# Moving the first batch's sink product from VectorE to GpSimd

## The chip, the core and the metric

The kernel runs on one core of one Trainium2 chip. A core has five engines that run side by side, each through its own list of instructions in order: TensorE (PE, matmuls; its weight loads are listed as PEld), VectorE (DVE), ScalarE (ACT), GpSimd (POOL) and SyncE (SP, here only issuing transfers). Engines wait for one another and for transfers (DMAs) by semaphores. The metric is the device time of one execution in microseconds; the lower, the better.

## The reference

Two stages, one behind the other. Attention with a sliding window and sink keys, for q, k and v of 4 batches, 8 heads, 768 positions and 64 elements a head:

```python
scores = scale * np.matmul(q, k.transpose(0, 1, 3, 2))
is_sink = pos[None, :] < int(n_sink)            # n_sink = 4
rel = pos[:, None] - pos[None, :]
in_window = (rel >= 0) & (rel < int(window))    # window = 128
keep = is_sink | in_window
scores = np.where(keep, scores, -1000000000.0)
a = np.exp(scores - max); a = a / (sum + 1e-09)
return np.matmul(a, v)
```

Then, on the heads put side by side (x: 4 x 768 rows of 512), a normalised two-layer network with a residual:

```python
xn = (x - mu) / np.sqrt(var + 1e-06) * g_ln
ch = np.maximum(xn @ w_ch1, 0.0) @ w_ch2        # 512 -> 2048 -> 512
return x + ch
```

## The kernel before

Rows are worked on in 24 tiles of 128 (six for each batch); two tiles make a chunk, so there are 12 chunks of 256 rows. For each chunk, k and q are loaded in natural layout, transposed, and multiplied to scores that hold keys along partitions (L679 in the first two chunks, L726 behind them); ScalarE takes the exponential (L685, L740), VectorE multiplies it with the window's mask (L688, L744; the first three tiles have the mask added on TensorE, L665), and TensorE multiplies with v (L774). v carries a column of ones, so that the 65th column of the product is the sum of the weights. VectorE takes its reciprocal (L787), scales (L789, which gives x), takes mean and variance (L793, L795) and subtracts the mean (L797, "centering": xc). xc is transposed (L810 on TensorE in the first three chunks, by DMA later), multiplied by the gain (L821) and goes through the first layer (L836 for chunk 0, tile by tile, in groups of 16 matmuls; L843 from chunk 1 on), a ReLU (L853 or L855) and the second layer (L872). L880 multiplies with the row's 1/sqrt(var), which GpSimd computes (L802, L803), and adds x.

The four sink keys of each head get their own small product from the second tile pair of a batch on: L693 (L730 later) multiplies q with a matrix of sink keys, ScalarE takes the exponential (L696, L748: the tile ps), and L769 multiplies it with vs, which has for each batch and head the sink rows of v in the rows that belong to that head, and zero in the others. vs is the product at L506. Its sources are vc, which holds the sink rows of v for all batches and a column of ones (eight small loads issued by SP at L502 fill it), and sel, the head selector: for each of 128 rows, which of 8 heads it belongs to. Both are read with stride 0 in one dimension, so that 128 x 65 and 128 x 8 values give 128 x 520. L506 is made four times, once for each batch; vs0 is needed first by tile 2's L769.

The order of the work isn't written out by hand. Each piece is entered with `P.op(name, {engine: (occupied, until ready)}, priority, ...)`; a planner (`Plan.run`) plays the pieces through with these costs, and each engine takes, of what can start within a small window, the piece of lowest priority. `nb` is a time before which a piece doesn't start; `dma` gives costs for a transfer and puts it on one of eight lanes of a planned queue. A piece with two engines goes to the one that would end it first: so the planner chooses where the transposed k and q are copied out of PSUM (L547, VectorE or ScalarE). The resulting order is emitted engine by engine. A change of one cost can therefore move other pieces; it does so in this case.

GpSimd's list around the place of the change: it issues the loads of the first chunks (L593, L541), the four quarters of the first layer's weights w1 (L514), the loads of chunk 2 (L627), the first two with k and the next two with q, and the quarters of the second layer's weights w2 (L517), with the rescales L802 and L803 of tiles 0 to 3 between them. A transfer issued by GpSimd waits until the one eight places before it has landed.

The priorities that the change touches are these lines, and the functions follow:

```python
P.op(f"vcd{h}", {"SP": (0.3, 0.3)}, 3.2 + 0.01 * h, ..., dma=HW_T)
P.op(f"vs{b}", {"DVE": dve(520)}, 2.0 if b == 0 else 48.0 * b - 20, ..., nb=12.0 if b == 0 else 40.0 * b)
```

Of the kernel before, what the change touches and what calls it, by code (L numbers as in the profile page):

```python
# [206 lines left out]
def dve(n, per=1.04):  # L207
    t = 0.067 + 0.001 * per * n
    return (t, t + 0.09)


def fix(occ, extra=0.09):
# [9 lines left out]
HW_T = (0.10, 0.8, 0.8)  # L222
# [3 lines left out]
NEVER = -1e9  # L226

PAR = dict(strict=40.0, win=0.4, tr=-8.0, sc=-5.0, sc1=-2.0, av=2.0, trx=9.0, by_dma=4, x_by_dma=3,
           w1p=(1.6, 2.6, 2.7, 2.8), pm=3, w2p=(4.5, 4.51, 4.52, 4.53), apart=2, by_tile=1, vp=(0.0, 0.1, 2.0, 2.1, 4.55, 4.56), ld1=0.05)


def general(tc, nc, slots, pairs, ones, ident_f, ident, w1, w2, mhalf, g_s, g_r, q, k, v, out, scale):
# [126 lines left out]
def kernel(  # L359
# [12 lines left out]
    nc = tc.nc  # L372
# [19 lines left out]
    P = Plan()  # L392
# [25 lines left out]
    def const(name, shape, dtype):  # L418
        return consts.tile(shape, dtype, name=name)
# [5 lines left out]
    sel = const("sel", [128, H], FP32)  # L425
    vc = const("vc", [128, B, 65], FP32)
    vs = [const(f"vs{b}", [128, H, 65], BF16) for b in range(B)]
# [11 lines left out]
    Bc = {n: Buf(n) for n in names}  # L439
    Bvs = [Buf(f"vs{b}") for b in range(B)]  # L440
# [6 lines left out]
    V, G = nc.vector, nc.gpsimd  # L447
# [35 lines left out]
    def negs(e):  # L483
# [15 lines left out]
         writes=[Bc["gt"]], dma=HW_T)  # L499
    for h in range(H):  # L500
        p0 = 32 * (h // 2) + NS * (h % 2)
        P.op(f"vcd{h}", {"SP": (0.3, 0.3)}, 3.2 + 0.01 * h, lambda e, h=h, p0=p0: nc.sync.dma_start(  # L502
            vc[p0:p0 + NS, :, 0:64], v[:, h, 0:NS, :].rearrange("b s d -> s b d")),
            reads=[Bc["vc"]], writes=[Bc["vcd"]], dma=HW_T)
    for b in range(B):
        P.op(f"vs{b}", {"DVE": dve(520)}, 2.0 if b == 0 else 48.0 * b - 20, lambda e, b=b: V.tensor_tensor(  # L506
            vs[b], vc[:, b, :].unsqueeze(1).to_broadcast([128, H, 65]),
            sel.unsqueeze(2).to_broadcast([128, H, 65]), op=ALU.mult),
            reads=[Bc["vcd"], Bc["vc"], Bc["sel"]], writes=[Bvs[b]], nb=12.0 if b == 0 else 40.0 * b)

    w1prio = PAR["w1p"]
    for c in range(4):
# [3 lines left out]
    for c in range(4):  # L516
        P.op(f"w2ld{c}", {"POOL": (0.75, 0.8)}, PAR["w2p"][c], lambda e, c=c: G.dma_start(  # L517
            w2[c], moe_w_ch2[512 * c:512 * (c + 1), :].rearrange("(t p) n -> p t n", p=128)),
            writes=[Bw2[c]], dma=SW_W)
# [376 lines left out]
    for c in range(NC):  # L896
        mlp(c)
        if c == PAR["x_by_dma"] - 1:
            for s in range(4):
                for j in range(NDM):  # L900
                    P.op(f"w1g{s}{j}", {"DVE": fix(0.26)}, 16.0 * c + 11.0 + 2 * s + 0.1 * j,
                         lambda e, s=s, j=j: V.tensor_scalar_mul(w1[s][:, j, :], w1[s][:, j, :], gt[:, j:j + 1]),
                         reads=[Bw1[s], Bc["gt"]], writes=[Bw1g[s]], after=last_use[s])

    def guard(e):
# [8 lines left out]
         reads=[pt_f], writes=[fl_b])  # L914
# [67 lines left out]
```

## Time and profile before

| what | value |
|---|---|
| runs: median (lowest to highest of 3) | 222.38 us (221.90 to 223.41) |
| the profiled execution's own time | 222.43 us |
| its span (first to last instruction) | 220.8 us |
| PE busy | 212.1 us (96%) |
| PEld busy | 144.6 us (65%) |
| DVE busy | 117.2 us (53%) |
| ACT busy | 108.8 us (49%) |
| POOL busy | 89.8 us (41%) |
| granted TensorE clock | 0.998 |
| L506 on DVE, 4 instructions | 0.68 to 0.70 us each |

The profile is that of one execution; its time is the span and 1.6 us around it. Busy times add up what each engine's instructions took; an engine that is busy half of the span may still be the one that all others wait for in some stretch. The page cuts the span into 40 slices of 5.5 us and gives each engine's busy share in tenths. "Idle before, releaser" behind a row says how long the engine stood still ahead of it and what ended that. Start times are counted from the start of the span. Rows of neighbouring instructions overlap a little, since an engine starts one before it has fully ended the last.

### The profile page before, as it was taken

To read this page: it belongs to the slowest core of one execution; us is meant where nothing else is said; L and a number is where in the kernel's file an instruction comes from. 1 tells how busy PE (TensorE), PEld (TensorE's weight loads), DVE (VectorE), ACT (ScalarE), POOL (GpSimd) and SP (SyncE) were. 2 spreads that over 40 slices of the span, in tenths; PEclk is the share of its full clock that TensorE was granted. 3 is DMA by queue.
4 is the path that set the end of the run, shared out by engine and by line. 5 is a ranking of instruction groups with operands and counts; after the bars stand their busy time and mean duration, and the time that the engine had idled before them with its cause. 6 is when DMAs were issued, how large, how long until landed. Compare 5 with 4: busy or idle time off the path is not lost.

```text
span 220.8 us, 5072 instructions
## 1 busy us (share of the span) xinstructions
PE 212.1 (96%) x2033; PEld 144.6 (65%) x2033; DVE 117.2 (53%) x269; ACT 108.8 (49%) x163; POOL 89.8 (41%) x130
## 2 busy tenths in 40 slices
PE   6888999999999999999999999999999999999991
PEld 2556975764964964964955965965955955966861
DVE  5499745585796725725706815716706706722011
ACT  3767565145546447445546546445545546531700
POOL 7987663798073480760460741740110110120000
PEclk9999999999999999999999999999999999999999
DMA  5999999999999896999997997998713511111012
GB/s 158 160 184 206 177 207 193 155 211 149 175 171 141 137 146 110 149 127 119 143 124 119 143 118 121 130 123 111 129 38 80 136 28 47 59 39 72 23 52 62
DMA packets 108576, 27.45 MB, mean 124 GB/s; under 512 B 99201, under 2 KB 105601, under 8 KB 108545
## 3 DMA queue, kind: packets, MB, share of 16 engines
q0 software_dynamic: 74944, 13.11, 79.6%
q1 hardware_dynamic: 32400, 13.28, 29.4%
q10 hardware_dynamic: 1200, 0.66, 1.1%
q8 instruction: 18, 0.29, 0.6%
q14 instruction: 14, 0.11, 0.1%
HBM read 27.30 MB, written 6.29 MB: 152 GB/s over the span
## 4 chain that ended last, share of the span: by engine, by line
PE 90%; DVE 4%; DMA 2%; ACT 1%; issue 1%; DVEq 0%
PE one L872 39%; PE one L843 35%; PE pair L726 5%; PE pair L774 4%; PE one L836 2%; DMA natf<-in_k_dram 2%; PE pair L769 1%; DVE st L793 1%; DVE x L789 1%; PE one L632 1%; PE one L576 1%; PE one L730 1%; PE pair L665 1%; DVE xnt L821 1%; DVE xc L797 1%
## 5 line engine op out<-in xcount | busy, mean ns | idle before, releaser
L872 PE MATMUL one<-w,h 128*128 128x512 bf16 (+1 forms) x400 | 89.0, 371 | 0.0
L853 ACT ACTIVATE h<-one 128x512 bf16<-128x512 f32 x95 | 56.8, 598 | 59.3 <-PE one L843 54.2
L843 PE MATMUL one<-xnt,w 128*128 128x256 bf16 x704 | 82.4, 273 | 0.0
L843 PEld LDWEIGHTS <-w 128*128 128x128 bf16 x704 | 67.4, 98 | 10.2
L872 PEld LDWEIGHTS <-h 128*128 128x128 bf16 x400 | 37.4, 98 | 38.6 <-issue 2.0
L744 DVE TENSOR_TENSOR pe<-pe,mask 128x1024 bf16<-128x1024 bf16 (+1 forms) x40 | 26.0, 650 | 55.6 <-ACT pe L740 54.7
L740 ACT ACTIVATE pe<-pair 128x1024 bf16<-128x1024 f32 (+1 forms) x40 | 36.2, 957 | 34.1 <-PE pair L726 31.8
L618 POOL DMA_DIRECT2D nat<-in_k_dram x16 | 14.3, 893 | 39.6 <-DMA kT<-nat 29.7
L880 DVE SCALAR_TENSOR_TENSOR ot<-one,st,x 128x512 f32<-128x512 f32 (+1 forms) x25 | 18.2, 726 | 22.6 <-PE one L872 22.4
L802 POOL TENSOR_SCALAR st<-st 128x1 f32<-128x1 f32 x24 | 7.5, 313 | 43.2 <-DVE st L795 42.1
L541 POOL DMA_DIRECT2D vn<-in_v_dram x24 | 21.9, 920 | 3.7 <-DMA w<-in_moe_w_ch_dram 3.1
L618 POOL DMA_DIRECT2D nat<-in_q_dram x16 | 14.8, 926 | 11.7 <-DMA qT<-nat 8.5
L793 DVE BATCH_NORM_STATS2 st<-x 128x6 f32<-128x512 bf16 x24 | 16.7, 695 | 0.8
L774 PEld LDWEIGHTS <-pe 128*128 128x128 bf16 x352 | 14.0, 97 | 2.3 <-ACT pe L685 0.6
L803 POOL TENSOR_TENSOR st<-st,mhalf 128x1 f32<-128x1 f32 x24 | 14.2, 593 | 2.0
L789 DVE TENSOR_TENSOR x<-pair,rec 128x512 bf16<-128x512 f32 x20 | 13.8, 691 | 0.7
L726 PEld LDWEIGHTS <-kT 64*128 64x128 bf16 x216 | 6.9, 94 | 8.5 <-issue 8.3
L774 PE MATMUL pair<-vn,pe 128*128 128x65 bf16 x296 | 12.2, 193 | 0.0
L726 PE MATMUL pair<-qT,kT 64*128 64x128 bf16 (+1 forms) x216 | 11.6, 238 | 0.0
L797 DVE TENSOR_SCALAR xc<-x,st 128x512 bf16<-128x512 bf16 x24 | 9.1, 377 | 0.9
L787 DVE RECIPROCAL rec<-pair 128x8 f32<-128x8 f32 x20 | 4.1, 204 | 9.9 <-PE pair L774 9.9
L685 ACT ACTIVATE pe<-pair 128x1024 bf16<-128x1024 f32 (+1 forms) x8 | 7.2, 918 | 3.6 <-PE pair L679 3.6
(84 smaller groups left out, 123.3 us busy)
## 6 DMA issues: line engine op xcount, KB each, us to landing
out_dram<-ot SPq DMA_DIRECT2D x23, 256.0 KB
w<-in_moe_w_ch_dram POOLq DMA_DIRECT2D x8, 512.0 KB, 12.3
vn<-in_v_dram POOLq DMA_DIRECT2D x24, 128.0 KB, 6.1
nat<-in_k_dram POOLq DMA_DIRECT2D x22, 128.0 KB, 5.8
nat<-in_q_dram POOLq DMA_DIRECT2D x22, 128.0 KB, 5.0
natf<-in_k_dram SPq DMA_DIRECT2D x2, 256.0 KB
natf<-in_q_dram ACTq DMA_DIRECT2D x2, 256.0 KB
xnt<-xc SPq DMA_TRANSPOSE x18
```

Source lines behind the costliest of these rows:

```text
L541: P.op(f"vld{t}", {"POOL": (0.87, 0.9)}, prio, lambda e: G.dma_start(bv.t[:, :, 0:64], v[b, :, 128 * r:128 * (r + 1), :].rearrange("h p d ...
L618: lambda e, nat=nat, ap=ap: G.dma_start(nat.t, ap), writes=[nat], dma=SW)
L726: nc.tensor.matmul(pp.t[:, h2, col:col + q1 - q0], lhsT=kt.t[rs, hp, k0:k0 + 128], rhs=qT.t[rs, hp, q0:q1], start=i == 0, stop=True, skip_ ...
L740: P.op(f"ex{c}{hp}", {"ACT": act(2 * n)}, d + 0.1 + 0.05 * j, lambda e, pp=pp, pb=pb: nc.scalar.activation(pb.t[:, :, 0:n], pp.t[:, :, 0:n ...
L744: V.tensor_mul(pb.t[:, :, 0:n], pb.t[:, :, 0:n], mm),
L774: nc.tensor.matmul(bank(h // 4)[:, 65 * (h % 4):65 * (h % 4) + 65], lhsT=part(h, n), rhs=vn_b[tv].t[:, h, :], start=(not R and h % 4 == 0 ...
L789: P.op(f"x{t}{run[0]}", {"DVE": dve(512 * share)}, dd + 0.11, lambda e, pv=pv, rc=rc, run=run: V.tensor_tensor(x.t[:, 256 * run[0]:256 * r ...
L793: P.op(f"bn{t}", {"DVE": fix(0.60)}, d + 0.12, lambda e: V.bn_stats(st.t[:, 8:14], x.t), reads=[x], writes=[st, mv])
L843: nc.tensor.matmul(ph.t[:, 256 * s:256 * s + 256], lhsT=w1[ht // 4][:, j, 128 * (ht % 4):128 * (ht % 4 + 1)], rhs=xnt.t[:, j, :], start=j ...
L853: nc.scalar.activation(hb.t, ph.t, AF.Relu)
L872: nc.tensor.matmul(pc.t[:, 0:wd], lhsT=(h1[2 * s + i].t[:, 128 * ii:128 * ii + 128] if by_tile else h1[ht // 2].t[:, 256 * (ht % 2) + 128 ...
L880: V.scalar_tensor_tensor(ot.t[:, sl], in0=pc.t[:, 0:wd], scalar=st.t[:, 16:17], in1=x.t[:, sl], op0=ALU.mult, op1=ALU.add),
```

## The change

For the first batch alone the product L506 is entered for GpSimd in place of VectorE, at a planned cost of 0.9 us (1.0 until its result can be used), with the same priority 2.0 and not before 13.0 us of the plan instead of 12.0. The products of the other three batches stay on VectorE. The eight small loads of the sink rows, still issued by SP in the same order, are planned as ready 5 us behind their issue, not before a time that grows by 0.55 us from one to the next, and no longer as pieces of the planned queue.

```diff
 PAR = dict(...
-           ... w2p=(4.5, 4.51, 4.52, 4.53), apart=2, by_tile=1, ...)
+           ... w2p=(4.5, 4.51, 4.52, 4.53), apart=2, vs0=(2.0, 13.0), by_tile=1, ...)
...
-        P.op(f"vcd{h}", {"SP": (0.3, 0.3)}, 3.2 + 0.01 * h, lambda e, h=h, p0=p0: nc.sync.dma_start(
+        P.op(f"vcd{h}", {"SP": (0.3, 5.0)}, 3.2 + 0.01 * h, lambda e, h=h, p0=p0: nc.sync.dma_start(
             vc[p0:p0 + NS, :, 0:64], v[:, h, 0:NS, :].rearrange("b s d -> s b d")),
-            reads=[Bc["vc"]], writes=[Bc["vcd"]], dma=HW_T)
+            reads=[Bc["vc"]], writes=[Bc["vcd"]], nb=3.5 + 0.55 * h)
     for b in range(B):
-        P.op(f"vs{b}", {"DVE": dve(520)}, 2.0 if b == 0 else 48.0 * b - 20, lambda e, b=b: V.tensor_tensor(
+        P.op(f"vs{b}", {"DVE": dve(520)} if b else {"POOL": (0.9, 1.0)}, PAR["vs0"][0] if b == 0 else 48.0 * b - 20, lambda e, b=b: (V if b else G).tensor_tensor(
             vs[b], vc[:, b, :].unsqueeze(1).to_broadcast([128, H, 65]),
             sel.unsqueeze(2).to_broadcast([128, H, 65]), op=ALU.mult),
-            reads=[Bc["vcd"], Bc["vc"], Bc["sel"]], writes=[Bvs[b]], nb=12.0 if b == 0 else 40.0 * b)
+            reads=[Bc["vcd"], Bc["vc"], Bc["sel"]], writes=[Bvs[b]], nb=PAR["vs0"][1] if b == 0 else 40.0 * b)
```

As built, the order of instructions changes in these places, all within the first 30 us: on GpSimd L506 stands between the two k loads of chunk 2 (L627), and the second quarter of w2 is issued ahead of tile 2's rescale (L802, L803) instead of behind it; on VectorE the place of L506 is taken by the copy of tile 3's transposed q (L547), which ScalarE made before, and both masks (L688) of tile 3 now stand ahead of tile 2's L821, where one stood behind it; on TensorE one group of 16 first-layer matmuls (L836, second quarter of w1) stands ahead of tile 2's transposes L810 instead of between the two halves of tile 3's values (L774). Behind that the lists are the same but for the PSUM buffers that some pieces use.

## The prediction

> **What bounds the kernel now.** I read the page's slices first, then the chain that ended last, then that chain between 12 and 22 us in order of time, then the timelines of POOL and PE there.
>
> ```profile
> span 220.8 us, 5072 instructions
> PE   6888999999999999999999999999999999999991
> ...
> PE 90%; DVE 4%; DMA 2%; ACT 1%; issue 1%; DVEq 0%
> ```
>
> TensorE (PE) is the bound: each slice is 5.5 us, the fourth digit is the last 8, and the chain is 90% PE. Where PE has gaps, before about 22 us, VectorE (DVE) leads. The chain between 12 and 22 us, merged (start, length, what):
>
> ```profile
> 13.35 0.78 DVE xc L797
> 14.13 0.04 issue
> 14.17 0.41 PE one L810 x4
> 14.58 0.02 issue
> 14.61 0.69 DVE xnt L821
> ...
> 17.20 0.70 DVE vs L506
> 17.90 0.60 DVE xnt L821
> 18.50 0.00 issue
> 18.50 0.19 DVE rec L787
> ...
> 20.67 0.35 DVE xc L797
> 21.03 0.61 DVE pe L688
> ```
>
> The product that the change moves (L506) lies on this chain, for 0.70 us. Next, POOL at 11 to 18 us and PE around its last gaps (start, length, line, idle before it and what ended that):
>
> ```profile
> 12.10 0.90 POOL L627 DMA_DIRECT2D nat<-in_k_dram  x1
> 13.15 0.88 POOL L627 DMA_DIRECT2D nat<-in_k_dram  x1 [0.15 <-issue]
> 14.10 0.22 POOL L802 TENSOR_SCALAR st<-st 128x1 f32<-128x1 f32 x1
> 14.41 0.57 POOL L803 TENSOR_TENSOR st<-st,mhalf 128x1 f32<-128x1 f32 x1
> ```
>
> ```profile
> 17.95 0.27 PE L769 MATMUL one<-vs,ps 128*128 128x260 bf16 x1 [0.32 <-DVE vs L506]
> ...
> 21.08 0.40 PE L810 MATMUL one<-ident,xc 128*128 128x128 bf16 x4 [0.43 <-DVE xc L797]
> 21.32 0.27 PE L769 MATMUL one<-vs,ps 128*128 128x260 bf16 x1
> 21.68 0.42 PE L774 MATMUL one<-vn,pe 128*128 128x65 bf16 x8
> 21.93 1.06 PE L836 MATMUL one<-xnt,w 128*128 128x128 bf16 x16
> 22.83 0.27 PE L769 MATMUL one<-vs,ps 128*128 128x260 bf16 x1
> ```
>
> Behind 22 us no PE row shows a wait worth naming. So the change is worth what it shifts the start of the solid PE stream, less what weights and tiles still in flight take back.
>
> **What goes from DVE.** The product starts at 17.20 and the next instruction at 17.82: 0.62 us. Its four semaphore waits (DVEq, 16.91 to 17.15) lie beside the centering of x in tile 1 (16.83 to 17.18), so they free nothing. In its place the built program puts the copy of tile 3's transposed q (L547), so far on ScalarE. The row of the same shape on DVE is 0.42 us. It fits between the end of the centering (17.18) and L821, which needs the transposes of that centred tile: PE started those at 17.24 and took 0.40, so L821 could start at 17.68 at best, by the 0.04 seen from PE's end to L821 at 14.57/14.61. So of the 0.62 us only 17.82 - 17.68 = 0.14 us comes free: **what is late next is the transpose.** ScalarE loses 0.58 us of copying, which nobody there waits for.
>
> **What moves on PE.** Planned with the shorter DVE chain, PE takes one first-layer group (16 matmuls L836 on the second weight quarter, 21.93 to 22.83, so 0.90 us) ahead of tile 2's transposes of the centred rows; before, it stood behind the first half of tile 3's attention values. There it fills the idle 0.43 us. It needs the second quarter of w1, issued at 9.83 and 10.2 us to landing: 20.0. I take the shift of the DVE chain as D (later is positive). Then the group ahead of it (19.58 now, 0.50 earlier without the wait for L506 and with its neighbours closer) ends at 19.98 + D, so this group runs at about 20.1 to 21.0 or, for D over 0.1, 19.98 + D to 20.88 + D. The transposes follow at 20.94 + D (21.08 now, less 0.14); they are held by the group by 0.1 at most.
>
> From there DVE's masks of tile 3 set the pace: the second starts at 22.14 - 0.74 = 21.40 + D, because the L821 that stood between the two now stands behind. With the row's 0.68 and 0.06 to PE, the second half of tile 3's values starts at 22.14 + D, and the next L836 group at 22.38 + D, against 23.18. Three groups (23.18 to 25.86, 2.68 us) end at 25.06 + D; tile 3's centering on DVE, 25.07 to 25.42 now, ends at 25.13 + D: 0.14 from above and 0.15 because the L787 at 23.45 need not wait for the values, which PE ended at 23.35. So its transposes start at 25.18 + D, against 25.86. **The solid stream is 0.68 - D earlier.**
>
> **What caps it.** The loads behind it do not come earlier: their queue is full, and each landing is set by the ones ahead. The two q loads for chunk 2 were issued at 15.69 and 16.66 and take 12.0 us: 27.7 and 28.65. PE reads the first at 28.27 now, so it can come 0.5 us earlier and no more. The last quarter of w1 (11.30 + 13.8 = 25.1) is read at 26.04 and would allow 0.9. So the gain ends at **0.5 us**. POOL issues these loads up to 1 us later, at nothing: they would sit behind the weights until 25 us anyway. w2 keeps over 10 us from issue to landing. The rescales (L802, L803) are read only at the first output, near 41 us.
>
> **What POOL's work costs.** In the built program L506 stands behind the issue of the first k load for chunk 2 (12.10 + 0.90), so it starts at about 13.1; its sources are there, issued on SP by 8.1. It is wanted by the L769 that ran at 17.95, so its length is hidden from PE even at 4 us. It isn't hidden from DVE. The centering of tile 0, in the chain at 13.35, took 0.77 where the median of the 24 of that line is 0.353. Beside it stood a POOL DMA issue, started at 13.15; the longest w1 scalings (L902) and one other centering also lie beside POOL DMA issues and end 1.0 us after the issue's start, 0.65 plus their own 0.35. So DVE waits where POOL holds something, and L506 now stands at just that place. If DVE waits to its end, the centering ends at 13.1 + d + 0.35 instead of 14.12, and D = d - 0.67, d being L506's time on POOL. **Gain = 0.68 - D = 1.35 - d.**
>
> The Trainium skill (SBUF — State Buffer, section "SBUF: two separate sides") says that GpSimd and a DVE instruction in a two-port mode exclude each other for a whole instruction, whichever starts first; the 0.77 agrees, though there the hold ended before the issue did.
>
> No POOL row has this shape. Below, d is at least 0.70, the same instruction on DVE. The nearest POOL row by size is the affine select (L452: 128 columns, 0.29): scaled to 520 columns, 1.18. Above, the one-column product (L803) takes 0.57; with twice the select's slope for two inputs, (0.29 - 0.10)/128 x 2 x 520 = 1.54, with 0.10 the one-column memset, that makes 2.1. I take the row nearest in size, **d = 1.2**: D = 0.53, gain 0.15. The ends are 0.5 (capped) and -0.75.
>
> The Trainium skill (GPSIMD Engine Reference, "Performance versus the Vector engine") gives about 2.6 cycles per element for a product of two tensors, at 1.2 GHz an estimate of 1.13 us for 520 before dispatch; with L802's 0.22 as dispatch the sum would be a gain of 0.0.
>
> **Sum.** The profiled execution took 222.43 us (span 220.8 and 1.6 around it), 0.05 from the median of the runs, 222.38. 222.43 - 0.15 = **222.3 us**.
>
> **The rivals.**
> 1. *DVE is not held* (the centering gets ahead of L506, or d is under 0.85). For it: 13.35 is only 0.25 after the assumed start, and the slow POOL DMA issue now leaves this place, which alone could give 0.42 back. Against it: the 0.77 row. The cap then decides: 222.43 - 0.5 = 221.9.
> 2. *Slower: POOL's product holds DVE too long.* One mechanism at one place, the centering at 13.35, and it decides from d = 1.35. At d = 2.1 it gives 222.43 + 0.75 = 223.2; if POOL's next DMA issue also gets in ahead of the waiting centering, another 0.65, 223.8. For it: 0.57 for one column is slow, and all behind 13.35 hangs on this instruction. It passes 1% only with d over 3.5.
> 3. *Nothing moves that counts*: PE waits for the second w1 quarter ahead of tile 2's transposes. That landing would have to slip from 20.0 by over 1 us to take the gain back; nothing ahead of it in its queue moves. 222.4.
>
> **How the numbers follow.** Chances: the forecast 0.40, DVE not held 0.22, POOL too long 0.33, the third 0.05. All but the far end of the second lie within 1% (2.2 us, about what a measurement of this kernel can tell from no change). The range takes d from 0.7 to 2.1, 221.9 to 223.2, and about 0.4 each way because the runs shown spread from 221.90 to 223.41: 221.5 to 223.6. Over 1% faster asks for more than the cap allows, 0.03; over 1% slower asks for a POOL product three times the nearest row, 0.07; within 1%, 0.90.
>
> **What would show it.** L506 on POOL at about 13.1 for 1.2 us; the centering at 13.35 drawn out to 1.3 us; the L547 copy in the old place of L506; a L836 group ahead of the transposes at 21.4; those of tile 3 at 25.7 instead of 25.86. Wrong would be: a centering of 0.35 us with the stream then stopped by q at 27.7, an L506 over 1.35 us, or a changed PE stream behind 30 us.

## The result and the profile after

| | before | after |
|---|---|---|
| median of 14 runs each (lowest to highest) | 222.64 us (221.60 to 223.41) | 221.80 us (221.47 to 222.56) |
| profiled execution: time, span | 222.43, 220.85 us | 221.66, 220.18 us |
| L506 of the first batch | DVE, 17.20 for 0.70 us | POOL, 13.00 for 1.13 us |

The ratio is 0.9966, 95% interval 0.9954 to 0.9978: **0.75 us less** (0.5 to 1.0), within 1% of no change. (The medians of the table lie 0.84 apart; the ratio's 0.75 is used from here on.) The forecast was 222.3 in a range of 221.5 to 223.6. The time lies in the range and within 1% of before, but the gain is five times the 0.15 us forecast. The page of the kernel after, in the parts shown of before:

```profile
span 220.2 us, 5075 instructions
...
PE   6889999999999999999999999999999999999992
...
PE 90%; DVE 6%; ACT 1%; issue 1%; DVEq 0%
```

TensorE is the bound as before, and the slices are nearly the same: changes of this size have to be looked for in the timelines. First POOL around the new place (start, length, line):

```profile
12.10 0.94 POOL L627 DMA_DIRECT2D nat<-in_k_dram  x1
13.00 1.13 POOL L506 TENSOR_TENSOR vs<-vc,sel 128x520 bf16<-128x520 f32 x1
14.01 0.94 POOL L627 DMA_DIRECT2D nat<-in_k_dram  x1
```

Then the chain that ended last, in order of time (start, length, what):

```profile
13.41 0.89 DVE xc L797
14.30 0.05 issue
14.35 0.41 PE one L810 x4
...
17.00 0.36 DVE xc L797
17.36 0.05 issue
17.41 0.41 PE one L810 x4
17.84 0.69 DVE xnt L821
```

The product has left this chain. Behind tile 1's centering (17.00) now stand tile 1's transposes (L810), which the prediction named as late next. The first centering is held for 0.53 us beyond its usual 0.35, to 14.29; before, it ended at 14.12. PE in the stretches where it had gaps:

```profile
19.27 2.00 PE L836 MATMUL one<-xnt,w 128*128 128x128 bf16 x32
21.10 0.39 PE L810 MATMUL one<-ident,xc 128*128 128x128 bf16 x4
...
25.43 0.40 PE L810 MATMUL one<-ident,xc 128*128 128x128 bf16 x4
...
28.30 1.04 PE L843 MATMUL one<-xnt,w 128*128 128x256 bf16 x8
```

The second group of 16 L836 stands ahead of tile 2's transposes, which start without the idle time of 0.43 us that they had. Tile 3's transposes start at 25.43 (25.86 before), the first L843 at 28.30 (28.54), and from there to the last matmuls the list runs 0.24 us earlier. The gain in the stream is thus 0.24 us, and the span is 0.67 shorter. The rest is at the end. The last three L880 on DVE, which make the last rows' output, before and then after:

```profile
212.76 0.75 DVE L880 SCALAR_TENSOR_TENSOR ot<-one,st,x 128x512 f32<-128x512 f32 x1 [9.69 <-PE one L872]
...
215.63 0.48 DVE L880 SCALAR_TENSOR_TENSOR ot<-one,st,x 128x256 f32<-128x256 f32 x1 [2.07 <-PE one L872]
...
216.49 0.48 DVE L880 SCALAR_TENSOR_TENSOR ot<-one,st,x 128x256 f32<-128x256 f32 x1 [0.38 <-PE one L872]
```

```profile
212.51 0.75 DVE L880 SCALAR_TENSOR_TENSOR ot<-one,st,x 128x512 f32<-128x512 f32 x1 [9.69 <-PE one L872]
...
215.03 0.48 DVE L880 SCALAR_TENSOR_TENSOR ot<-one,st,x 128x256 f32<-128x256 f32 x1 [1.72 <-PE one L872]
...
216.25 0.48 DVE L880 SCALAR_TENSOR_TENSOR ot<-one,st,x 128x256 f32<-128x256 f32 x1 [0.73 <-PE one L872]
```

The first and the third of the three move with the stream, by 0.25 and 0.24 us; the second moves by 0.60. It starts 0.40 us behind the end of the last semaphore wait that stands ahead of it before, and 0.04 behind it after; the wait that it carries itself had been met at 194.8 us before and 194.6 after, so no semaphore explains the 0.40. From the end of the last L880 to the end of the span it is 3.88 us before and 3.45 after, 0.43 less. The output transfer behind the second one is issued 0.59 us earlier (215.55 for 216.14); that it therefore gets less in the way of the last one is likely, but not shown. Nothing in the prediction speaks of this, and it is more than half of the gain seen in the profile.

### The profile page after: what moved, and what is told of

Its sections match the earlier page's. It is cut to its first block, busy times and chain, and to the rows that moved or that the text cites. A ratio compares the mean times of both kernels' runs of the same rounds, so it can differ in the third digit from the quotient of the medians.

```text
span 220.2 us, 5075 instructions
## 1 busy us (share of the span) xinstructions
PE 212.4 (96%) x2033; PEld 144.6 (66%) x2033; DVE 117.2 (53%) x269; ACT 108.2 (49%) x162; POOL 92.7 (42%) x131
## 4 chain that ended last, share of the span: by engine, by line
PE 90%; DVE 6%; ACT 1%; issue 1%; DVEq 0%
PE one L872 39%; PE one L843 35%; PE pair L726 5%; PE pair L774 4%; PE pair L938 2%; PE pair L769 1%; DVE st L793 1%; DVE x L789 1%; DVE xnt L821 1%; DVE xc L797 1%; PE one L632 1%; PE one L836 1%; PE one L810 1%; PE one L730 1%; PE pair L665 1%; PE one L576 1%
## 5 line engine op out<-in xcount | busy, mean ns | idle before, releaser
L843 PE MATMUL one<-xnt,w 128*128 128x256 bf16 x704 | 82.4, 273 | 0.0
L843 PEld LDWEIGHTS <-w 128*128 128x128 bf16 x704 | 67.4, 98 | 10.2
L618 POOL DMA_DIRECT2D nat<-in_k_dram x16 | 16.2, 1015 | 37.5 <-DMA kT<-nat 32.5
L880 DVE SCALAR_TENSOR_TENSOR ot<-one,st,x 128x512 f32<-128x512 f32 (+1 forms) x25 | 18.2, 726 | 22.6 <-PE one L872 22.5
L802 POOL TENSOR_SCALAR st<-st 128x1 f32<-128x1 f32 x24 | 7.2, 298 | 40.9 <-DVE st L795 39.6
L803 POOL TENSOR_TENSOR st<-st,mhalf 128x1 f32<-128x1 f32 x24 | 14.5, 603 | 2.0
L774 PEld LDWEIGHTS <-pe 128*128 128x128 bf16 x352 | 14.0, 97 | 2.0 <-ACT pe L685 0.6
L789 DVE TENSOR_TENSOR x<-pair,rec 128x512 bf16<-128x512 f32 x20 | 13.8, 690 | 0.7
L774 PE MATMUL pair<-vn,pe 128*128 128x65 bf16 x296 | 12.2, 193 | 0.0
L797 DVE TENSOR_SCALAR xc<-x,st 128x512 bf16<-128x512 bf16 x24 | 9.8, 410 | 0.9
L787 DVE RECIPROCAL rec<-pair 128x8 f32<-128x8 f32 x20 | 4.0, 201 | 9.9 <-PE pair L774 9.9
```

Source lines behind the costliest of these rows:

```text
L618: lambda e, nat=nat, ap=ap: G.dma_start(nat.t, ap), writes=[nat], dma=SW)
L774: nc.tensor.matmul(bank(h // 4)[:, 65 * (h % 4):65 * (h % 4) + 65], lhsT=part(h, n), rhs=vn_b[tv].t[:, h, :], start=(not R and h % 4 == 0 ...
L789: P.op(f"x{t}{run[0]}", {"DVE": dve(512 * share)}, dd + 0.11, lambda e, pv=pv, rc=rc, run=run: V.tensor_tensor(x.t[:, 256 * run[0]:256 * r ...
L843: nc.tensor.matmul(ph.t[:, 256 * s:256 * s + 256], lhsT=w1[ht // 4][:, j, 128 * (ht % 4):128 * (ht % 4 + 1)], rhs=xnt.t[:, j, :], start=j ...
L880: V.scalar_tensor_tensor(ot.t[:, sl], in0=pc.t[:, 0:wd], scalar=st.t[:, 16:17], in1=x.t[:, sl], op0=ALU.mult, op1=ALU.add),
```

## The experiments

All ratios are to the kernel before, run beside on the same chip, with 95% intervals. Where an edit moves a piece, it does so in the finished order of the plan, which leaves all other pieces in their places: `move(order, (piece, engine, other, place))` puts the piece on that engine, ahead of (minus) or behind (plus) the other one. In the plan, vs0 is the first batch's L506, kld20 and kld21 are the two k loads of chunk 2, rs0 is tile 0's rescale (L802, L803), xc1 is tile 1's centering, evk3 and evq3 are the copies of tile 3's transposed k and q (L547).

**again.** The kernel after, unchanged, with a second profile.

> The changed kernel as it is, once more, for a second profile of it. In the first, PE's stream stood 0.24 us earlier than before from 30 us on, while the medians differ by 0.84 us. If the rest is a matter of how far single executions differ (loads for chunk 2 landed 0.2 to 0.9 us later in the profile after than in that of before), a second profile shows other landings: q at about 27.7 and PE earlier by 0.4 us than the kernel before. If the rest is a gain behind the last matmul, the stream stands again at about 0.24 and the time from the last L872 to the end of the span is shorter by 0.4 again. Ratio 0.9966 +- 0.001 by both.

Measured: 0.9968 (0.9956 to 0.9981), 221.91 us. L506 takes 1.15 us on POOL from 13.01, but the centering beside it starts at 13.79 and takes 0.53: it ends at 14.32, only 0.03 from where it ended in the first profile, though it began 0.38 later. So the end of the hold is set by POOL, and its size by when DVE arrives.

**engine_only.** The order of before, with nothing but the first L506 moved to GpSimd between the two k loads.

```diff
-        P.op(f"vs{b}", ..., lambda e, b=b: V.tensor_tensor(
+        P.op(f"vs{b}", ..., lambda e, b=b: (V if b else G).tensor_tensor(
...
-    order = P.run()
+    order = P.run(); move(order, ('vs0', 'POOL', 'kld21', -0.5))
```

> The kernel before with nothing but L506 of the first batch moved to GpSimd, at the same place as in the changed kernel; all other lists as before. Theory 1 (the gain comes from the L836 group that the new order puts into PE's gap ahead of tile 2's transposes): the centering at 13.4 takes 0.88, the 0.62 us freed on DVE is used up by that and by waiting for the transposes, and the L836 group behind tile 2's transposes goes on as before; PE's first three-group stretch starts at 23.1 (23.18 before), ratio 0.9997 (0.999 to 1.001). Theory 2 (the gain is the 0.62 us that DVE no longer spends): ratio as for the changed kernel, 0.9966.

Measured: 0.9978 (0.9966 to 0.9991), 222.02 us, between the two expectations (0.9997 and 0.9966). PE still stands idle ahead of tile 2's transposes, longer than before, since all ahead of them is done sooner:

```profile
21.15 0.40 PE L810 MATMUL one<-ident,xc 128*128 128x128 bf16 x4 [0.68 <-DVE xc L797]
```

So the stream gains little here, and yet 0.49 us is gone by the ratio. In its profile the second-last L880 starts 0.04 us behind its last wait, as in the kernel after.

**order_only.** The order of after, with L506 back on DVE behind tile 1's centering, and the copy of tile 3's q back on ScalarE.

```diff
-        ... lambda e, b=b: (V if b else G).tensor_tensor(
+        ... lambda e, b=b: V.tensor_tensor(
...
-    order = P.run()
+    order = P.run(); move(order, ('vs0', 'DVE', 'xc1', 0.5), ('evq3', 'ACT', 'evk3', 0.5))
```

> The order of the changed kernel on TensorE, with L506 back on DVE between tile 1's centering and L821, and the copy of tile 3's q back on ScalarE: so the order alone, without GpSimd. Theory 1: the L836 group fits into PE's gap from 20.2 on as in the changed kernel, tile 3's transposes start at 25.5 (25.86 before, 25.43 in the changed kernel), ratio 0.997 to 0.998. Theory 2: DVE spends its 0.62 us as before, ratio 1.000.

Measured: 0.9976 (0.9965 to 0.9987), 222.18 us: 0.53 us without a product on GpSimd. PE has no gap ahead of tile 2's transposes any more:

```profile
19.72 1.96 PE L836 MATMUL one<-xnt,w 128*128 128x128 bf16 x32
21.52 0.39 PE L810 MATMUL one<-ident,xc 128*128 128x128 bf16 x4
```

Here the second-last L880 has the 0.40 us of before, and the stretch from the last L880 to the end is 3.95.

**twice.** After, with the first batch's product made twice in a row on GpSimd (the same values into the same place), to double the time for which POOL could hold DVE.

```diff
-    ... lambda e, b=b: (V if b else G).tensor_tensor(...)
+    ... lambda e, b=b: [(V if b else G).tensor_tensor(...) for _ in range(1 if b else 2)]
```

> The changed kernel with the product on GpSimd made twice, one behind the other (the second has the same result). If DVE's centering at 13.4 waits while GpSimd works on the product, it takes 0.88 + 1.1 = 2.0 us, all behind it comes 1.1 us later, and the load of q no longer holds PE: 222.7 us where the changed kernel has 221.8, ratio 1.000 to 1.002. If the 0.88 has another cause (the DMA issue ahead, or the one behind), the centering stays at 0.9 us and the time at that of the changed kernel, since the product itself is wanted only at 17.6.

Measured: 0.9956 (0.9942 to 0.9971), 221.69 us, not slower than after, where a hold to the end of both would have given about 1.001. POOL, then DVE:

```profile
13.80 2.21 POOL L506 TENSOR_TENSOR vs<-vc,sel 128x520 bf16<-128x520 f32 x2
```

```profile
14.12 0.91 DVE L797 TENSOR_SCALAR xc<-x,st 128x512 bf16<-128x512 bf16 x1
```

The first of the two products ends at 14.87 and the second starts at 14.95. The centering ends at 15.03, 0.16 us behind the end of the first and 0.98 ahead of the end of the second, at 16.01. DVE got in between the two products. So the hold is for one POOL instruction, and a second one right behind it doesn't add to it.

**before_again, after_plus1, before_minus1.** These ask what makes the 0.36 us at the end. The count of instructions on DVE ahead of that L880 was the suspect: after has one separate semaphore wait fewer on DVE than before (54 for 55), so that the second-last L880 is number 319 of DVE's list, counted from 0 with waits and branches, where it was 320. (The trace leaves out a branch near the head of the list; in its rows the numbers are one lower.) before_again is the kernel before once more, as a control. after_plus1 fills a constant twice on DVE, which puts the number back to 320; before_minus1 lets GpSimd fill one, ahead of tile 0's rescale, which makes it 319.

In the kernel after:

```diff
-    constant("ones_f", "DVE", ..., lambda e: V.memset(ones_f, 1.0), ...)
+    constant("ones_f", "DVE", ..., lambda e: [V.memset(ones_f, 1.0) for _ in range(2)], ...)
```

In the kernel before:

```diff
-    constant("mhalf", "DVE", ..., lambda e: V.memset(mhalf, -0.5), ...)
+    constant("mhalf", "DVE", ..., lambda e: G.memset(mhalf, -0.5), ...)
-    order = P.run()
+    order = P.run(); move(order, ("mhalf", "POOL", "rs0", -0.5))
```

> The kernel before, once more, as a control and for a second profile of it. Ratio 1.000 (0.9985 to 1.0015) by all theories. If the second last L880 (the first half of the last tile) is late because of where it stands in DVE's list, it starts again 0.44 us behind its last semaphore wait, and from the end of the last L880 to the end of the span it takes again 3.9 us; if that was chance, 0.05 to 0.1 and about 3.5.

> The changed kernel with one instruction more on DVE, a memset of one column at 4.1 us made twice, where DVE is idle to 6.4. Theory A (part of the gain lies in the tail: the changed kernel has one DVE instruction fewer, so that the second last L880 is instruction 319 of DVE's list and not 320, and 320 has to wait for code): that L880 starts 0.4 us later, the tail is 3.9 us instead of 3.5, ratio 0.9985 (0.9975 to 0.9995). Theory B (the tail differs by chance, the whole gain stands in the stream): nothing changes, 0.9967.

> The kernel before with one instruction fewer on DVE: the one-column memset of mhalf is made on GpSimd, behind its second k load. L506 and all orders are as before. Theory A: the second last L880 starts 0.05 to 0.1 us behind its wait, the tail is 3.5 us, ratio 0.9982 (0.997 to 0.999), without anything of the change. Theory B: ratio 1.000.

Measured: before_again 0.9998 (0.9985 to 1.0011); after_plus1 0.9980 (0.9968 to 0.9992), 222.17 us; before_minus1 0.9986 (0.9972 to 1.0000), 222.15 us. One instruction more on DVE takes 0.0013 of the gain away (0.9967 was expected without an effect), and one fewer gives the kernel before 0.0014: 0.3 us in both directions. The second-last L880 in after_plus1 and then in before_minus1:

```profile
215.51 0.48 DVE L880 SCALAR_TENSOR_TENSOR ot<-one,st,x 128x256 f32<-128x256 f32 x1 [2.07 <-PE one L872]
```

```profile
215.64 0.48 DVE L880 SCALAR_TENSOR_TENSOR ot<-one,st,x 128x256 f32<-128x256 f32 x1 [1.72 <-PE one L872]
```

The idle time ahead of it goes with the count, 2.07 or 1.72, in after's order as in before's. The profile names the matmuls as what ended it, which the swap shows to be wrong in the first of the two.

**clear_place.** After, with L506 and the second k load's issue put behind tile 0's rescale on GpSimd, so that nothing on POOL stands beside the first centering.

```diff
-    order = P.run()
+    order = P.run(); move(order, ('vs0', None, 'rs0', 0.4), ('kld21', None, 'rs0', 0.5))
```

> The changed kernel with L506 and the second k load of chunk 2 put behind the first rescale on GpSimd, so that nothing of GpSimd stands beside the centering at 13.4. By the hold, the centering takes 0.35 there, up to 0.5 us less than in the changed kernel, and L506 runs at about 15. Theory 1 (the loads cap the gain: w1 at 20.1, q at 27.9): tile 2's transposes stay at 21.1 and the stream from 30 us on stays within 0.15 us of the changed kernel, ratio 0.9967 (0.996 to 0.9975). Rival (DVE's chain still sets the pace): the stream comes 0.3 to 0.5 us earlier, ratio 0.995.

Measured: 0.9972 (0.9959 to 0.9985), 221.82 us, no better than after. The centering takes 0.35 (13.67), L506 runs at 14.74 for 1.05, so the hold is gone. But now the second L836 group reads its weights at 20.00, 0.04 us behind their landing at 19.95, and PE reads the first q of chunk 2 at 27.84, 0.04 behind its landing at 27.79. In this profile the first L843 stands at 28.08, 0.22 us earlier than in after, between the two expectations, and the span is 219.8; but it is the profile of the shortest of the eleven executions (221.27), and the median shows no gain. Part of what the hold had cost is paid to the loads.

**order_minus1.** order_only, with GpSimd filling the constant as in before_minus1: the whole sum, with no product on GpSimd.

```diff
-    order = P.run()
+    order = P.run(); move(order, ('vs0', 'DVE', 'xc1', 0.5), ('mhalf', 'POOL', 'rs0', -0.5), ('evq3', 'ACT', 'evk3', 0.5))
```

> The order of the changed kernel on TensorE with L506 on DVE and the q copy on ScalarE, as in order_only, and one DVE instruction fewer (mhalf's memset on GpSimd), as in before_minus1: both gains without moving L506 to GpSimd. If the gain of the changed kernel is the sum of order (0.9976) and instruction count (0.9986), this has all of it: ratio 0.9963 (0.995 to 0.9975), the second last L880 0.05 us behind its wait. If GpSimd's part is needed, 0.9976 to 0.998.

Measured: 0.9961 (0.9945 to 0.9976), 221.82 us; expected was 0.9963. The order and the count make as much as the whole change, with L506 on DVE.

**before_less_w1, after_less_w1.** The two kernels without the load of the last quarter of w1, to empty the queue ahead of the q loads.

```diff
-    w1 = [const(f"w1_{c}", [128, NDM, 512], BF16) for c in range(4)]
+    w1 = [const(f"w1_{c}", [128, NDM, 512], BF16) for c in range(3)]; w1 = w1 + w1[2:3]
...
-        P.op(f"w1ld{c}", ..., lambda e, c=c, sl=sl: G.dma_start(
+        P.op(f"w1ld{c}", ..., lambda e, c=c, sl=sl: c < 3 and G.dma_start(
```

> The kernel before without the load of the fourth quarter of w1 (the third is used in its place, so the result isn't the reference's): 0.5 MB less ahead of the k and q loads for chunk 2, which land some 2.5 us earlier (q at 25.3 instead of 27.9). It has 319 DVE instructions ahead of the second last L880, so its tail is the short one. The stream is set by DVE's chain as before, so it gains the tail alone: ratio 0.9986 (0.997 to 1.0).

> The changed kernel without the load of the fourth quarter of w1, as in before_less_w1. If q's landing holds the changed kernel, PE's read of q isn't late any more (it followed the landing by 0.04 us in two profiles of the changed kernel), and the first L843 comes 14.2 us behind the start of the first centering, less what GpSimd holds of that (14.9 and 14.4 in the changed kernel): ratio 0.996 (0.9945 to 0.997), 0.5 us under before_less_w1. If not, 0.9967.

Measured: before_less_w1 0.9981 (0.9966 to 0.9997), 222.25 us, expected 0.9986; after_less_w1 0.9975 (0.9960 to 0.9989), 222.31 us, expected 0.9960, a miss. Its profile shows q in time, but tile 1's centering is held instead (0.71 us at 17.10, beside the issue of the second q load). And its end is not the short one. This kernel has one wait fewer still on DVE (53), so the second-last L880 is number 318 and the last one number 320. Now it is the last that starts late, though its own wait had been met at 209.9 (the chain that ended last, in order of time):

```profile
216.44 0.02 DVEq L880
216.46 0.40 issue
216.86 0.48 DVE ot L880
```

"issue" is time in which DVE waited for nothing that the profile shows; in after and in before it takes 0.04 at this place. The expectation did not reckon with this; 0.36 us would be the 0.0015 that were missed, but the hold of tile 1's centering in the profile is as large. The two kernels' times don't settle it, so what the late loads cost in the median stays open.

### All profiles side by side

The stream's own length is taken here from the start of the first centering to the first L843, less what the first two centerings took above 0.35 us each.

| kernel | first centering, start / us | L506 | stream's own length | second-last L880 behind its wait | end of last L880 to end of span |
|---|---|---|---|---|---|
| before | 13.35 / 0.77 | DVE | 14.77 | 0.40 | 3.88 |
| before_again | 14.43 / 0.35 | DVE | 14.77 | 0.40 | 3.95 |
| before_minus1 | 13.84 / 0.35 | DVE | 14.66 | 0.04 | 3.62 |
| engine_only | 14.04 / 0.38 | POOL, 1.11 us | 14.58 | 0.04 | 3.46 |
| order_only | 13.49 / 0.47 | DVE | 14.27 | 0.40 | 3.95 |
| order_minus1 | 14.27 / 0.35 | DVE | 14.24 | 0.04 | 3.34 |
| after | 13.41 / 0.88 | POOL, 1.13 us | 14.36 | 0.04 | 3.45 |
| again | 13.79 / 0.53 | POOL, 1.15 us | 14.20 | 0.04 | 3.58 |
| after_plus1 | 14.17 / 0.50 | POOL, 1.08 us | 14.10 | 0.40 | 4.30 |
| twice | 14.12 / 0.91 | POOL, 2.21 us for two | 14.17 | 0.04 | 3.60 |
| clear_place | 13.67 / 0.35 | POOL, 1.05 us | 14.40 | 0.04 | 3.29 |
| before_less_w1 | 13.52 / 0.35 | DVE | 14.78 | 0.04 | 3.56 |
| after_less_w1 | 14.03 / 0.35 | POOL, 1.06 us | 14.18 | 0.04 (the last: 0.40) | 3.56 |

By means of the rows, the stream's own length is 14.74 in the four with before's order and L506 on DVE. It falls by 0.49 us with the order alone (14.25), by 0.16 with the engine alone (14.58), and by 0.58 with both where no load is late (14.16, the mean of again, after_plus1, twice and after_less_w1; in again q landed at 27.88, just ahead of its read at 27.92). In after and clear_place PE waits for w1 and q, which takes 0.20 and 0.24 back. The last two columns change together, whatever the order: with 0.40 the end takes 3.88 to 4.30 us, with 0.04 it takes 3.29 to 3.62. Counted from the end of the last wait ahead of the last L880, after_less_w1 belongs to the long ones: 4.41 to 4.83 us with an L880 that is late by 0.40, 3.81 to 4.15 without.

No version beat the changed kernel beyond the intervals: twice has 0.9956, order_minus1 0.9961, after 0.9966, clear_place 0.9972.

## Why the prediction was right in its class and wrong in its size

**The closure.** In the profiled executions the stream's own length is 0.42 us shorter (14.77 to 14.36, the loads' waits taken in); the hold grew from 0.42 to 0.53 (0.11), and the first centering started 0.07 later: 0.24, the shift seen on PE. With 0.43 at the end that makes the 0.67 us of span. In the ratio, 0.75 us is 0.3 at the end, by the two count swaps, and about 0.45, what is left, in the stream. That the time fell into the range owes something to luck: it is 0.1 below the 221.9 that the sum's best end gave, inside only by what was added for the spread of the runs, and the 0.3 at the end was in no term.

**From DVE 0.14 us: right.** The copy of q took the place (17.36 for 0.42), and L821 came at 17.84, where the sum 17.68 + D gives 17.85 with the D measured. The engine alone gave 0.16.

**The order on PE, 0.68 - D: right in its mechanism, 0.08 too large.** With the measured D of 0.17, the steps give tile 2's transposes at 21.11 (21.10 measured) and the next L836 group at 22.55 (22.47), but tile 3's transposes at 25.35 where they came at 25.43. The term that was not there is the 0.15 at L787: it was to come earlier since it need not wait for the values. In both kernels it starts 0.08 us behind the end of the L789 ahead of it (22.95 + 0.42 and 23.45; 22.89 + 0.42 and 23.39). A separate semaphore wait stands between the two in DVE's list. In the kernel after it had been met at 22.65, and L787 still did not start before L789 had ended. Where none stands there, as at 18.66 and 19.00 in the kernel after, L787 starts before L789 has ended.

**L506 on POOL, 1.2 us: right.** It took 1.13, and 1.05 to 1.15 in the other profiles. The row nearest in size, scaled by columns, was the one to take; the one-column product, with its slope doubled, was far off. The Trainium skill (GPSIMD Engine Reference, "Performance versus the Vector engine") gave 1.13 for the elements alone, and the trace agrees with that for the whole row, with no dispatch to add.

**The hold, D = 0.53: this is the step that failed in size, at 0.17.** DVE was held, as forecast, and at the place forecast. The centering did not wait for the end of L506's row, though: with 0.35 of work it began to work at 13.94, 0.19 us before that row ended at 14.13. In all four other profiles with a held first centering and the product on POOL it is 0.19 as well: again (13.97 and 14.16), engine_only (14.07 and 14.26), after_plus1 (14.32 and 14.51) and the first product of twice (14.68 and 14.87). The two rows overlap by 0.2 to 0.8 us there, so a centering that only ran more slowly beside POOL would not come out at the same 0.19 each time. The forecast put L506 at 13.1, and it came at 13.00; with L506 0.07 us shorter and this 0.2 earlier, that accounts for the 0.36. The prediction's own row had shown it: beside the POOL issue that ended at 14.03, the centering worked from 13.77. It was used for the issue and not carried over to the product. The Trainium skill's rule that the two exclude each other (SBUF — State Buffer, "SBUF: two separate sides") agrees with the traces in that DVE is blocked, for one instruction at a time, as twice shows; that it lasts for the whole instruction does not agree to the last 0.2 us of the row, as far as the ends of POOL's rows can be trusted.

**The hold is also not the same in each execution.** The profile before that the sum was made against has its first centering at 13.35. In before_again it starts at 14.43 and is not held at all. The difference arises in the first 8 us, shown here in before and then in before_again:

```profile
5.55 0.61 PE L576 MATMUL one<-ident,natc 128*128 128x128 bf16 x4
```

```profile
5.57 1.06 PE L576 MATMUL one<-ident,natc 128*128 128x128 bf16 x4
```

The same four matmuls at the same time take 0.61 or 1.06 us. The record in which the clock is granted in full starts 5.1 us into the span in before, and 7.77 in before_again. Between them DVE's chain moves by 1.1 us against POOL's list, which does not move with it. In the other profiles, too, the first centering starts later where that record does, from 5.70 and 13.41 (after) to 7.43 and 14.27 (order_minus1); only close neighbours are swapped, by 0.05 us at most. before_minus1 is the exception, with 4.76 and 13.84: there PE stands idle for 0.71 us until 7.67, for a tile of k whose load landed at 6.75. So the late clock goes with the shift in twelve of the 13 profiles, and the landing of a first load can shift it too. No run changed either on purpose. The Trainium skill (TensorE: Matmul & The Clock Gate, "Part 1: The HAM clock gate (the "warmup" mystery)") says that the gate watches windows which run free of the kernel's start, and that the number of slow matmuls at the start differs between runs; the traces agree with the second, and of the windows no run here shows anything. So a price of a collision taken from one profile is the price of that execution.

**The cap: right in kind.** PE read q at 28.06, 0.04 us behind its landing at 28.02, in after, and 0.04 behind 27.79 in clear_place. The landing foreseen at 27.7 came 0.3 us later in after, so the cap was 0.2 and not 0.5 (28.27 to 28.06): that is why the 0.43 us at tile 3's transposes are only 0.24 at the first L843.

**The rivals.** The first, DVE not held, named 221.9, which is near the time measured, but its mechanism is not what the profile shows: the centering was held. The second, POOL too long, falls, since L506 took less than 1.35 and the hold does not last to its end. The third falls, since PE read the second quarter of w1 at 20.20, as it landed (20.15), and tile 2's transposes were not late.

**The end: missing altogether.** The prediction said that behind 22 us no PE row shows a wait worth naming, and looked at PE alone there. The wait is DVE's, in the last 6 us, and the change took it away by its count of instructions. That the count decides is shown in both directions; between order_only and order_minus1, too, it made 0.0015. None of these three differences is clear of its interval by itself, but they agree in sign and size, and the profiles show the wait come and go with them. after_less_w1 adds that the 0.40 us belongs to the place in the list and not to the second-last L880: there the last one is number 320, and it is the late one. Why the place decides is not shown. A guess is that DVE's next instructions are being fetched, with number 320 the first that needs them: 320 is a multiple of 64, and in every trace an 8 KB transfer of the instruction queue starts between 214.7 and 215.8 us. But that transfer is there with and without the delay, and in after_plus1 it ends at 215.68, 0.17 us after the late L880 has started. The Trainium skill (Runtime: NRT & Kernel Launch, "Instruction fetch mechanics") says that engines fetch their lists in blocks while they run, mostly hidden; if this is such a crossing, it cost 0.36 us at a point where nothing was left to hide it. The blocks of that page hold 256 instructions, and 320 is no multiple of 256. Number 256 itself starts 0.03 to 0.04 us behind the end of the instruction ahead of it in all 13 traces, so not every multiple of 64 shows such a delay.

## What to carry to other kernels

A small piece taken off the chain is worth what the next late thing allows, here 0.14 to 0.16 us of 0.62; the reordering that came with it was worth three times as much, and could have been had without moving the product. Price a collision between two engines from several executions, since engines that don't follow the same early waits shift against each other by more than the collision lasts. And where an edit changes the number of instructions on an engine, look at the last microseconds of that engine: 0.3 us of the 0.75 came from there, and one constant filled on another engine gave it too.

## What was not expected of the hardware

- The second-last L880 starts 0.40 us behind its last wait when it is number 320 of DVE's list and 0.04 when it is 319; where the last L880 is number 320, it is the late one. An execution is 0.3 us longer or shorter for it.
- DVE gets in 0.19 us before the end of a GpSimd product's row, in five profiles, and between two products that follow each other directly (2.21 us for both; the centering ended 0.16 us behind the first).
- The full clock came between 4.8 and 7.8 us into the span, and the first centering between 13.35 and 14.43.
